# A gated recurrence and a cosine-gated layer on one core: order of sums, products and copies around the matmuls, and of the last group's tiles

## The chip, the core and the metric

The kernel runs on one NeuronCore of a Trainium2 chip. The engines work side by side, each through its own instructions in order, and wait for one another by semaphores: PE (TensorE, matmuls; its weight loads are shown apart as PEld), DVE (VectorE), ACT (ScalarE), POOL (GpSimd) and SP (SyncE, which here only issues DMAs). The metric is the device time of one execution in microseconds (us); lower is better. Three runs of the kernel before took 646.26, 646.23 and 644.99 us, the median is 646.23.

## The reference

```python
mag = np.sqrt(a_re * a_re + a_im * a_im)
scale = np.minimum(mag, 0.999) / (mag + 1e-06)
a_re_n, a_im_n = (a_re * scale, a_im * scale)
for t in range(S):                        # 768 steps, (batch 4, heads 8, 48 x 48 state)
    ar, ai = (a_re_n[:, :, t, :, None], a_im_n[:, :, t, :, None])
    new_re = ar * S_re - ai * S_im
    new_im = ar * S_im + ai * S_re
    kv = np.einsum('bhd,bhe->bhde', k[:, :, t], v[:, :, t])
    S_re, S_im = (new_re + kv, new_im)
    y[:, :, t] = np.einsum('bhd,bhde->bhe', q[:, :, t], S_re)
x = y.transpose(0, 2, 1, 3).reshape(3072, 384)
h = x @ w_in                              # 384 x 2048
g = h * np.cos(h)
out = g @ w_out                           # 2048 x 384
```

A recurrence with a complex decay per step and channel is followed by a layer with a cosine gate.

## The kernel before

The 3072 rows are cut into 24 chunks of 128 steps, two chunks to a group, so there are 12 groups g = 0 to 11; three groups make a batch, at whose start the recurrence begins anew (g = 0, 3, 6, 9). The first two groups and the weights' conversion are written out in order by hand; from group 2 on a loop over n runs, and only this loop and what follows it are touched here. One pass of it holds work of three groups at once:

- for group n + 1 the decays: `g_log`/`log_steps` (squares, logarithm, exponentials), `p_powers` (running sums of the logs on PE, `lgs`, then four exponentials on ACT into `lg` and `pair`, "the powers" below), `g_angle` (a table load and the arctangent on `tan`), `g_carry` (adds the angle of the chunk before, on DVE; not at a batch's start), `g_split` (`hi` on ACT, `lo` on DVE), `g_phase` (running sums of the angles on PE, `phs`), `g_trig`, `g_stack` (`ks`, `qs`), and `f_transpose` (`tr` on DVE, then through DRAM as `moved` into `kT` and `qT`). `p_end` halves the tile `end` and folds it into `least`, for a check at the program's end;
- for group n the scores `sc`, their masking into `atm` on DVE, the outputs `yp`, the state, and then the layer's first matmul in eight tiles of 256 columns of `w_in` (`first`, `mm1`);
- for group n - 1 the layer's second matmul, done as seven products of quarter matrices instead of eight (`seventh`, named a11, a12, s2, a22, s1, s3, s4 in this order on PE, 16 matmuls each). The mixes `s` and `gate<-gate` that they need are made on DVE. a11, s2, s1 and s4 add up in one PSUM tile, `sum`; after a11, s2, s1 (and s4, but in the last group) ACT copies its content out to `ot`, and the next of these products may write the tile only when that copy has read it. "The third sum's copy" is the one behind s2 (p == 3).

Five of the eight tiles (3 to 7) are computed as three products of rounded matrices, "three-product tiles": tiles 4 and 5 from group 3 on, 6 and 7 from group 4, 3 from group 5. They need `xT` cut into an upper part (`cut`, copied to `xh`), a lower part `xl` and a sum `xx` (`x_halves`: upper, lower, apart). For such a tile PE writes `hp` (xh times wh plus xl times wl) and `hb` (xx times wx); ACT copies `hb`, scaled, into `gate` (`cross_out`); DVE adds it onto `hp` (`whole_sum`, in the trace `hp<-hp,gate`); then come sine and square on ACT (`gate_sine`; `junk` is the square's output) and the product on DVE (`gate_product`, in the trace `gate<-hp,gate`). A plain tile has the sine, the square and the product alone. The gate part of a three-product tile is held back until the matmuls of the tile behind it are issued ("held").

What sets the order: `weave` sorts the steps of a pass by the place given to each between 0 and 1; a scheduler then orders each engine's instructions by that order and by readiness; `behind(a, b)` puts a behind b on their engine without a semaphore, and `chain` strings all instructions given to it on one engine, so the special functions on ACT stand in the order in which they are issued. PSUM tiles of `hp` rotate over three places, `hb`, `sc` and others over five.

Of the kernel before, what the change touches and what calls it, by code (L numbers as in the profile page):

```python
# [487 lines left out]
def fast_path(ctx, tc, q, k, v, a_re, a_im, moe_w_in, moe_w_out, out, least, odd, wide,  # L488
# [12 lines left out]
    G = 2  # L501
# [41 lines left out]
    def behind(ins, other):  # L543
        tc.add_manual_dep(ins.ins, other.ins.name, mybir.DependencyInfo(
            mybir.DependencyClass.NoSync, mybir.DependencyReason.DATA))
# [343 lines left out]

    def p_end(g, i, n):  # L890
        end = X[g]["end"][:, ds(i * H, n * H)]
        vector.tensor_scalar(out=end, in0=end, scalar1=-0.5, scalar2=None, op0=ALU.mult)
        low = least[:, ds(i * H, n * H)]
        vector.scalar_tensor_tensor(out=low, in0=end, scalar=LEAST, in1=low,
                                    op0=ALU.is_ge, op1=ALU.min)
# [265 lines left out]
    def x_halves(g):  # L1161

        x = X[g]

        def all_of():
            return x["xT"].rearrange("p c g t -> p (c g t)")

        def upper():
            whole = all_of()
            for name, tag in ("xx", "lg"), ("xl", "lo"), ("xh", "rs"):  # L1170
                x[name] = gt.tile([C, G * DM], F32R, tag=tag, name=name)
            x["cut"] = ft.tile([C, G * DM], F32, tag="yT", name="cut", bufs=1)
# [12 lines left out]
        def apart():  # L1185
            apart_ = vector.scalar_tensor_tensor(
                out=x["xx"], in0=x["xl"].bitcast(F32), scalar=-SHIFT,
                in1=x["cut"], op0=ALU.mult, op1=ALU.add)
            if g + 1 < NG:
                behind(apart_, x["product"])  # L1190

        return upper, lower, apart

    def three(g, jp):
        return g >= FROM.get(jp, NG)
# [67 lines left out]
    def mm1_gate(g, jp):  # L1263
        gate_sine(g, jp)
        gate_product(g, jp)

    def mm1(g, jp, last):

        mm1_sums(g, jp)
        if three(g, jp):  # L1270
            cross_out(g, jp)
        if "held" in X[g]:
            mm1_gate(g, X[g].pop("held"))
        if three(g, jp):
            X[g]["held"] = jp
            whole_sum(g, jp)
        else:
            mm1_gate(g, jp)
        if last:
            if g + 2 < NG:  # L1280
                X[g + 2]["steps"] = log_steps(g + 2, 0, G)
                next(X[g + 2]["steps"])
            if "held" in X[g]:
                mm1_gate(g, X[g].pop("held"))
# [68 lines left out]
    def seventh(g, p, part):  # L1353
# [19 lines left out]
        if g == NG - 1:  # L1373
            c12 = rest
        if p in (0, 3, 5) or p == 6 and not alone:
            late["scalar"] = scalar.mul(out={0: c11, 3: c21, 5: c22, 6: c12}[p], in_=ps, mul=scale)
        if g == NG - 1 and p == 5:
            scalar.mul(out=c12, in_=ps, mul=scale)
        for part_ in {1: [c11], 2: [c21], 4: [c21, c22], 6: [c12] * alone}.get(p, []):
# [44 lines left out]
    def keys(g):  # L1424

        if not 0 <= g < NG:
            return
        for i, n in spans(g):
            yield lambda i=i, n=n: g_trig(g, i, n)
            yield lambda i=i, n=n: (g_stack(g, i, n), p_end(g, i, n))  # L1430
            for name in "kT", "qT":
                if g >= PEG:
                    yield lambda i=i, n=n, name=name: f_transpose(g, i, n, name)
# [5 lines left out]
        return [lambda i=i: p_powers(g, i) for i in range(G)]  # L1439

    def prods(g):
        if not 0 <= g < NG:
            return
        if g not in (1, 2):
            yield from powers(g)
            yield lambda: g_angle(g, 0, G)
        if g <= PEG:
            yield lambda: (g_carry(g), g_split(g))
            yield lambda: (p_even(g, 0, G), p_apply(g, 0, G))
        else:  # L1450
            yield lambda: p_around(g)
# [36 lines left out]
    def first(g):  # L1488
        late_ = [jp for jp in THREE if FROM[jp] == g + 1]
        order = late_ + [jp for jp in range(NJ // 2) if jp not in late_]  # L1490
        if g == NG - 1:
            order = 0, 4, 1, 5, 2, 6, 7, 3
        return [lambda jp=jp: mm1(g, jp, jp == order[-1]) for jp in order]

    def second(g, i):
# [293 lines left out]
    for n in range(2, NG):  # L1789
        turned_keys, plain = list(keys(n + 1)), n == PLAIN  # L1790
        split = x_halves(n) if any(three(n, jp) for jp in THREE) else ()
        guard_ = list(guarded(n - 1, per)) if n > 2 else []
        convert = [lambda jp=jp: halves(jp) for jp in THREE if FROM[jp] == n + 1]
        if split and n < NG - 1:
            X[n + 1]["upper"] = split[0]
        weave((mixes(n - 1, 2, 4), 0.0, 0.08), (logs(n + 1), 0.0, 0.02), (chunks(n), 0.0, 0.36),
              (upper[2:] if plain else [], 0.0, 0.2), (products(n - 1, 0, 2 + (n < NG - 1)), 0.0, 0.365),
              (mixes_again(n - 1, "s3"), 0.06, 0.18), (mixes_again(n - 1, "s2"), 0.19, 0.27),
              (angles(n + 1), 0.2695, 0.2699), (prods(n + 1), 0.2701, 0.2735), (second(n - 1, 1), 0.36, 0.5),
              (mixes_again(n - 1, "s4"), 0.37, 0.48),  # L1800
              (products(n - 1, 2 + (n < NG - 1), 7), 0.4, 0.56),
              (convert[0:1], 0.82, 0.82), (convert[1:2], 0.93, 0.93),
              (phases(n + 1), *((0.472, 0.476) if plain else (0.476, 0.484))),
              (turned_keys[0:1], 0.5, 0.5), (split[0:1] if n == NG - 1 else [], 0.525, 0.525), (turned_keys[1:2], 0.53, 0.53),
              (turned_keys[2:3], 0.56, 0.56), (turned_keys[3:4], 0.6, 0.6), ([lambda: rest_of(n - 1)], 0.605, 0.605), (split[1:2], *[0.61 if n < NG - 1 else 0.53] * 2),
              (split[2:3], *[0.65 if n < NG - 1 else 0.54] * 2), (last_quarter() if plain else [], 0.9, 1.0), (first(n), 0.56, 1.0),
              (mixes(n, 0, 2 + (n == NG - 1)), 0.98 if convert else 0.92, 1.0 if n < NG - 1 else 0.97), (guard_[0:1], 0.1, 0.1),
              (guard_[1:2], 0.26, 0.26), (guard_[2:3], 0.47, 0.47))
    checked = verdict(late, temp)

    def judged():
        late["tensor"] = tail["tensor"]
        next(checked, None)

    weave(([judged], 0.0, 0.0), (mixes(NG - 1, 3, 4), 0.01, 0.1),
          (mixes_again(NG - 1, "s3"), 0.05, 0.15), (mixes_again(NG - 1, "s2"), 0.16, 0.26), (mixes_again(NG - 1, "s4"), 0.3, 0.4),
          (products(NG - 1, 0, 7), 0.0, 1.0), ([judged], 0.58, 0.6), ([judged], 0.76, 0.8))
    assert not guards
# [92 lines left out]
```

## Time and profile before

| | |
|---|---|
| median of three runs | 646.23 us |
| the profiled execution's own time | 647.06 us |
| its span, first to last instruction | 645.2 us |
| mean granted clock of PE | 0.997 |
| PE busy | 627.5 us, 97% |
| DVE busy | 529.7 us, 82% |
| ACT busy | 450.6 us, 70% |
| table load ahead of the arctangent, n = 7 and n = 8 | starts at 392.64 and 442.20 us |

All times of the trace are microseconds from the span's start. A row of the order of time gives start, duration, engine, line, operation, output <- inputs, shapes, how many instructions were merged, and in brackets how long the engine was idle before and what ended the wait. Many instructions share lines 681, 692 and 712, which are helpers that record every operation, so rows are told apart by their tiles. Two passes of the loop are 49.6 us apart by the table loads of the last row. A wait for several semaphores is put down to the one that came last by the profile.

### The profile page before, as it was taken

What the parts mean: (1) busy time and instruction counts of PE and PEld (TensorE: products, weight loads), DVE (VectorE), ACT (ScalarE), POOL (GpSimd) and SP (SyncE); (2) the same over time, 40 slices, a digit from 0 to 9 for tenths busy, and PEclk for the clock granted to TensorE, in tenths of its full rate; (3) what the DMA queues carried; (4) which work ended last, traced back from release to release, by engine and by line L of the source; (5) the groups of instructions that cost most, each with busy time, mean ns of one, the idle gap of its engine ahead of it and who ended that gap; (6) DMA issues with size and microseconds to landing.
All of it is one profiled execution on the core that took longest, in us unless ns stands there. A gap on an engine that the chain in (4) does not pass through costs nothing.

```text
span 645.2 us, 11446 instructions
## 1 busy us (share of the span) xinstructions
PE 627.5 (97%) x4321; PEld 573.0 (89%) x4321; DVE 529.7 (82%) x856; ACT 450.6 (70%) x812; POOL 30.3 (5%) x53
## 2 busy tenths in 40 slices
PE   8999999999999999999999999999999999999987
PEld 6788867777899999999999999999999899999987
DVE  6999989869798799898799799788889889973261
ACT  7888687285696696697598588588588589552430
POOL 4010200000010000000000000000000000000000
PEclk9999999999999999999999999999999999999989
DMA  9968655725926926946946945855865863641001
GB/s 229 247 190 217 195 172 117 179 49 135 208 65 158 245 74 157 224 112 148 236 108 148 221 124 148 199 145 140 187 165 130 190 162 109 150 97 50 25 2 31
DMA packets 232923, 94.94 MB, mean 147 GB/s; under 512 B 208701, under 2 KB 221246, under 8 KB 232858
## 3 DMA queue, kind: packets, MB, share of 16 engines
q1 hardware_dynamic: 225320, 68.51, 46.7%
q0 software_dynamic: 5824, 25.50, 12.0%
q8 instruction: 36, 0.59, 0.4%
q10 hardware_dynamic: 1714, 0.11, 0.2%
q14 instruction: 29, 0.24, 0.1%
HBM read 69.28 MB, written 24.81 MB: 146 GB/s over the span
## 4 chain that ended last, share of the span: by engine, by line
PE 46%; ACT 23%; DMA 12%; DVE 9%; issue 6%; SPq 2%; ACTq 0%; DVEq 0%
PE hp L692 16%; PE op L692 11%; PE sum L692 6%; PE sc L692 3%; PE hb L692 3%; DVE tr L681 2%; ACT rs L712 2%; ACT junk L681 2%; ACT tan L712 2%; PE yp L692 2%; DMA row<-lg 2%; ACT lg L712 2%; DMA k<-in_k_dram 2%; ACT raw L681 2%; ACT yT L681 2%
## 5 line engine op out<-in xcount | busy, mean ns | idle before, releaser
L692 PE MATMUL hp<-xT,w_in 128*128 128x256 f32 (+1 forms) x684 | 146.9, 372 | 0.7 <-DVE gate L681 0.7
L692 PEld LDWEIGHTS hp<-xT,w_in 128*128 128x128 f32 x684 | 125.9, 190 | 18.5 <-DVE gate L681 1.1
L712 ACT ACTIVATE gate<-hp,half_pi_b 128x512 f32<-128x512 f32 x96 | 65.9, 687 | 62.8 <-PE hp L692 40.8
L692 PE MATMUL op<-w_out,gate 128*128 128x192 f32 (+1 forms) x464 | 104.8, 377 | 0.0
L692 PEld LDWEIGHTS op<-w_out,gate 128*128 128x128 f32 x464 | 80.4, 193 | 16.7 <-issue 1.9
L692 PE MATMUL sum<-w_out,gate 128*128 128x192 f32 x304 | 54.9, 328 | 2.6 <-DVE gate L681 2.6
L681 ACT ACTIVATE junk<-hp 128x512 bf16<-128x512 f32 x96 | 56.7, 590 | 0.0
L681 DVE TENSOR_TENSOR gate<-hp,gate 128x512 f32<-128x512 f32 x55 | 37.6, 686 | 19.9 <-ACT junk L681 19.6
L692 PEld LDWEIGHTS sum<-w_out,gate 128*128 128x128 f32 x304 | 49.2, 190 | 2.9 <-DVE gate L681 2.9
L681 DVE SCALAR_TENSOR_TENSOR gate<-hp,gate 128x512 f32<-128x512 f32 x41 | 28.3, 691 | 27.3 <-ACT junk L681 27.2
L692 PE MATMUL sc<-qT,kT 96*128 96x128 f32 x384 | 48.9, 276 | 0.6 <-ACT gate L681 0.3
L692 PEld LDWEIGHTS sc<-qT,kT 96*128 96x128 f32 x384 | 46.8, 192 | 2.4 <-issue 0.6
L692 PE MATMUL hp<-xh,wh 128*128 128x256 f32 x246 | 44.2, 288 | 0.0
L692 PE MATMUL hp<-xl,wl 128*128 128x256 f32 x246 | 42.5, 281 | 0.0
L692 PE MATMUL hb<-xx,wx 128*128 128x256 f32 x246 | 35.7, 286 | 2.2 <-DVE xx L681 2.2
L681 DVE TENSOR_TENSOR gate<-gate 128x256 f32<-128x256 f32 x80 | 32.6, 418 | 5.4 <-PE op L692 4.8
L692 PEld LDWEIGHTS hp<-xh,wh 128*128 128x128 f32 x246 | 35.8, 189 | 0.5
L681 DVE TENSOR_TENSOR atm<-sc,causal 128x512 f32<-128x512 f32 x48 | 32.0, 683 | 4.8 <-PE sc L692 4.8
L681 ACT ACTIVATE ot<-sum 128x192 f32<-128x192 f32 x39 | 12.5, 320 | 32.5 <-PE sum L692 32.5
L692 PE MATMUL yp<-atm,v 128*48 128x128 f32 x352 | 34.0, 277 | 0.8 <-DVE atm L681 0.8
L692 PEld LDWEIGHTS hp<-xl,wl 128*128 128x128 f32 x246 | 34.8, 188 | 0.0
L681 DVE TENSOR_TENSOR hp<-hp,gate 128x512 f32<-128x512 f32 x41 | 28.4, 692 | 7.8 <-ACT gate L681 7.4
(163 smaller groups left out, 1262.3 us busy)
## 6 DMA issues: line engine op xcount, KB each, us to landing
moved<-tr SPq DMA_DIRECT2D x20, 768.0 KB
raw<-in_moe_w_in_dram POOLq DMA_DIRECT2D x16, 768.0 KB, 5.7
raw<-in_moe_w_out_dram POOLq DMA_DIRECT2D x16, 768.0 KB, 5.0
kT<-moved SPq DMA_DIRECT2D x40, 192.0 KB
qT<-moved SPq DMA_DIRECT2D x10, 768.0 KB
k<-in_k_dram SPq DMA_DIRECT2D x24, 192.0 KB
q<-in_q_dram SPq DMA_DIRECT2D x24, 192.0 KB
v<-in_v_dram SPq DMA_DIRECT2D x24, 192.0 KB
```

Of the source, the lines that this page charges most:

```text
L681: ins = getattr(self.engine, op)(**kw)
L692: chain(nc.tensor.matmul(out, **kw), "tensor")
L712: chain(nc.scalar.activation(func=func, **kw))
```

## The change

It has five parts.

- `mm1`: for a held three-product tile the sine and square are issued as before, but the next tile's sum (`whole_sum`) is issued ahead of the held tile's product, and the product is put behind that sum.
- `x_halves` and the loop: `apart` (xx) is no longer put behind the first product, and stands right behind `lower` (place 0.612 instead of 0.65). `p_end` moves from the stacking step to place 0.615, behind xx.
- `seventh`: the third sum's copy is chained on ACT in passes up to n = 10; to this end `prods` is split, and `carries` with the arctangent, the carry and the split is issued at 0.336 instead of 0.27.
- `first`: the last group's tiles run in the order 0 3 1 4 2 5 6 7 instead of 0 4 1 5 2 6 7 3.
- The mixes of the last group: two of the four are placed ahead of the loop's end instead of three.

```diff
     def p_end(g, i, n):
         end = X[g]["end"][:, ds(i * H, n * H)]
-        vector.tensor_scalar(out=end, in0=end, scalar1=-0.5, scalar2=None, op0=ALU.mult)
+        halved = vector.tensor_scalar(out=end, in0=end, scalar1=-0.5, scalar2=None, op0=ALU.mult)
+        if g > 0 and "apart" in X[g - 1]:
+            behind(halved, X[g - 1]["apart"])
...
-            if g + 1 < NG:
-                behind(apart_, x["product"])
+            x["apart"] = apart_
...
         if three(g, jp):
             cross_out(g, jp)
-        if "held" in X[g]:
-            mm1_gate(g, X[g].pop("held"))
+        held = X[g].pop("held", None)
+        if held is not None:
+            gate_sine(g, held)
         if three(g, jp):
             X[g]["held"] = jp
             whole_sum(g, jp)
-        else:
+        if held is not None:
+            gate_product(g, held)
+            if three(g, jp):
+                behind(X[g]["product"], X[g]["whole"])
+        if not three(g, jp):
             mm1_gate(g, jp)
...
-            late["scalar"] = scalar.mul(out={0: c11, 3: c21, 5: c22, 6: c12}[p], in_=ps, mul=scale)
+            late["scalar"] = copied = scalar.mul(out={0: c11, 3: c21, 5: c22, 6: c12}[p], in_=ps, mul=scale)
+            if p == 3 and g < NG - 2:
+                chain(copied)
...
-            yield lambda i=i, n=n: (g_stack(g, i, n), p_end(g, i, n))
+            yield lambda i=i, n=n: (g_stack(g, i, n), g > PEG or p_end(g, i, n))
...
     def prods(g):
+        return powers(g) if 0 <= g < NG else []
+
+    def carries(g):
         if not 0 <= g < NG:
             return
-        if g not in (1, 2):
-            yield from powers(g)
-            yield lambda: g_angle(g, 0, G)
+        yield lambda: g_angle(g, 0, G)
...
         if g == NG - 1:
-            order = 0, 4, 1, 5, 2, 6, 7, 3
+            order = 0, 3, 1, 4, 2, 5, 6, 7
...
-              (angles(n + 1), 0.2695, 0.2699), (prods(n + 1), 0.2701, 0.2735), (second(n - 1, 1), 0.36, 0.5),
+              (angles(n + 1), 0.2695, 0.2699), (prods(n + 1), 0.2701, 0.2735), (carries(n + 1), 0.336, 0.34), (second(n - 1, 1), 0.36, 0.5),
...
-              (split[2:3], *[0.65 if n < NG - 1 else 0.54] * 2), (last_quarter() if plain else [], 0.9, 1.0), (first(n), 0.56, 1.0),
-              (mixes(n, 0, 2 + (n == NG - 1)), 0.98 if convert else 0.92, 1.0 if n < NG - 1 else 0.97), (guard_[0:1], 0.1, 0.1),
+              (split[2:3], *[0.612 if n < NG - 1 else 0.54] * 2), ([lambda: p_end(n + 1, 0, G)] if n + 1 < NG else [], 0.615, 0.615), (last_quarter() if plain else [], 0.9, 1.0), (first(n), 0.56, 1.0),
+              (mixes(n, 0, 2), 0.98 if convert else 0.92, 1.0 if n < NG - 1 else 0.97), (guard_[0:1], 0.1, 0.1),
```

How the instructions stand on the engines follows from the scheduler as well. On DVE, in a pass of the loop from the cut of `xT` on (`gate<-hp,gate` with two operands is a plain tile's product or, as SCALAR_TENSOR_TENSOR, a three-product tile's; `hp<-hp,gate` is a sum), before:

```order
L681 TENSOR_SCALAR cut<-xT 128x768
L681 TENSOR_SCALAR end<-end 96x16
L681 SCALAR_TENSOR_TENSOR least<-end,least 96x16
L681 TENSOR_TENSOR gate<-hp,gate 128x512
L681 TENSOR_TENSOR xl<-xT,cut 128x768
L681 TENSOR_TENSOR gate<-hp,gate 128x512
L681 SCALAR_TENSOR_TENSOR xx<-xl,cut 128x768
L681 TENSOR_TENSOR gate<-hp,gate 128x512
L681 TENSOR_TENSOR hp<-hp,gate 128x512
L681 SCALAR_TENSOR_TENSOR gate<-hp,gate 128x512
L681 TENSOR_TENSOR hp<-hp,gate 128x512
```

and now, in the same place:

```order
L681 TENSOR_SCALAR cut<-xT 128x768
L681 TENSOR_TENSOR gate<-hp,gate 128x512
L681 TENSOR_TENSOR xl<-xT,cut 128x768
L681 SCALAR_TENSOR_TENSOR xx<-xl,cut 128x768
L681 TENSOR_SCALAR end<-end 96x16
L681 TENSOR_TENSOR gate<-hp,gate 128x512
L681 SCALAR_TENSOR_TENSOR least<-end,least 96x16
L681 TENSOR_TENSOR gate<-hp,gate 128x512
L681 TENSOR_TENSOR hp<-hp,gate 128x512 x2
L681 SCALAR_TENSOR_TENSOR gate<-hp,gate 128x512
```

xx has passed one product, the two instructions on `end` have left the way of xl, and the second sum has passed the first three-product tile's product.

On ACT, in a pass behind the powers, with the arctangent as `tan<-tan` and the third sum's copy as `ot<-sum` (a minus is before, a plus now):

```order
 L712 ACTIVATE lg<-lgs 128x384
 L712 ACTIVATE pair<-lgs 128x384
-L708 ACT_TABLE_LOAD
-L712 ACTIVATE tan<-tan 128x768
-L681 ACTIVATE ot<-sum 128x192
+L681 ACTIVATE ot<-sum 128x192
+L708 ACT_TABLE_LOAD
+L712 ACTIVATE tan<-tan 128x768
 L733 ACTIVATE hi<-tan 128x768
```

The copy has passed the table load and the arctangent; nothing else moved there.

On PE the rows are the same in kind all through. In the last group, behind the tiles, the first product (a11, into `sum`) and the second (a12, into `op`) read these gates, by number, where 5631 (before) and 5629 (now) is the gate of the tile that is computed last:

```order
 L692 MATMUL sum_5656<-w_out_125,gate_5470 128x192 x2
 L692 MATMUL sum_5656<-w_out_125,gate_5511 128x192 x2
 L692 MATMUL sum_5656<-w_out_125,gate_5550 128x192 x2
-L692 MATMUL sum_5656<-w_out_125,gate_5631 128x192 x2
-L692 MATMUL op_5675<-w_out_125,gate_5497 128x192 x2
+L692 MATMUL sum_5656<-w_out_125,gate_5497 128x192 x2
 L692 MATMUL op_5675<-w_out_125,gate_5536 128x192 x2
 L692 MATMUL op_5675<-w_out_125,gate_5575 128x192 x2
 L692 MATMUL op_5675<-w_out_125,gate_5598 128x192 x2
+L692 MATMUL op_5675<-w_out_125,gate_5629 128x192 x2
```

The last tile's gate has moved from the end of the first product to the end of the second.

More of the change, by code (lines that the diff above doesn't have):

```diff
@@ L1813, in judged @@
         next(checked, None)
-    weave(([judged], 0.0, 0.0), (mixes(NG - 1, 3, 4), 0.01, 0.1),
+    weave(([judged], 0.0, 0.0), (mixes(NG - 1, 2, 4), 0.0, 0.1),
           (mixes_again(NG - 1, "s3"), 0.05, 0.15), (mixes_again(NG - 1, "s2"), 0.16, 0.26), (mixes_again(NG - 1, "s4"), 0.3, 0.4),
```

## The prediction

> **What bounds the kernel now.** I read the page first, then who waits for whom on the weight-load track, then the order of time around each wait.
>
> ```profile
> span 645.2 us, 11446 instructions
> PE 627.5 (97%) x4321; PEld 573.0 (89%) x4321; DVE 529.7 (82%) x856; ACT 450.6 (70%) x812; POOL 30.3 (5%) x53
> ```
>
> PE is busy for 627.5 of 645.2 us, and the change leaves every matmul in place, so at most the 17.7 us of its idle time and time at a low clock can go. Which idle stretches there are, the weight loads (PEld, issued by the same sequencer) show best:
>
> ```profile
> PEld sum L692 <- ACT ot L681: 3.9, 5, 1.3
> PEld hb L692 <- DVE xx L681: 3.4, 6, 0.7
> PEld sum L692 <- DVE gate L681: 2.9, 1, 2.9
> PEld yp L692 <- DVE atm L681: 1.8, 4, 0.6
> PEld sc L692 <- ACT gate L681: 0.5, 1, 0.5
> ```
>
> The first three rows, 10.2 us, are the three places that the change edits: the third sum's copy `ot` (five waits), `xx` (six), and the last gate of the last group (one). Of the fourth row two of four waits, about 0.9 us, lie in the loops n = 6 and 9, which the change reaches; the fifth is the start of n = 11.
>
> **The tail (order 0 3 1 4 2 5 6 7).** In order of time, then the page's granted clock over the span and one stretch with it (the column behind POOL), then the page's groups for a sine, a square and a mix:
>
> ```profile
> 618.10 2.11 PE L692 MATMUL sum<-w_out,gate 128*128 128x192 f32 x12
> 620.00 0.69 DVE L681 TENSOR_TENSOR hp<-hp,gate 128x512 f32<-128x512 f32 x1
> 622.08 0.69 DVE L681 SCALAR_TENSOR_TENSOR gate<-hp,gate 128x512 f32<-128x512 f32 x1
> 622.83 0.92 PE L692 MATMUL sum<-w_out,gate 128*128 128x192 f32 x4 [2.62 <-DVE gate L681]
> 623.59 4.44 PE L692 MATMUL op<-w_out,gate 128*128 128x192 f32 x16
> 630.46 2.76 PE L692 MATMUL op<-t_a,gate 128*128 128x192 f32 x16
> PEclk9999999999999999999999999999999999999989
> 623.86:627.27 3.41, 3.41 (x13) 3.41 (x12) 1.25 (x3) 0.26 (x1) 0.00 (x0) 0.50 0.02 0
> L712 ACT ACTIVATE gate<-hp,half_pi_b 128x512 f32<-128x512 f32 x96 | 65.9, 687 | 62.8 <-PE hp L692 40.8
> L681 ACT ACTIVATE junk<-hp 128x512 bf16<-128x512 f32 x96 | 56.7, 590 | 0.0
> L681 DVE TENSOR_TENSOR gate<-gate 128x256 f32<-128x256 f32 x80 | 32.6, 418 | 5.4 <-PE op L692 4.8
> ```
>
> The first product takes 12 matmuls and then sits 2.62 us until tile 3's gate, the last of eight, is there at 622.77. One microsecond after PE resumes, the clock falls to 0.50 for 3.41 us, and a product of 16 matmuls lasts 4.44 instead of 2.76 us: 1.68 us more. In the new order the first product reads gates 0 to 3, all early, and runs through; the second reads gate 7 only in its last quarter. That quarter starts 16 + 12 matmuls behind 618.10; at 2.60 us for 16 (the n = 7 rows below, 32 in 5.20) this is 622.65. The last gate also comes earlier: its sum (0.69) no longer waits for the held product. The last tile's matmuls end about where the product starts, so its sum ends near 619.0, sine (0.69) and square (0.59) take until 620.3, and the product until about 621.4 with two mixes in its queue. That is 1.2 us of room. Behind it stand the mixes for the third product (0.42 each, some seven of them, to about 624.4), whose last quarter is read at 618.10 + 44/16 × 2.60 = 625.25. So the gap goes and nothing replaces it: **2.62 + 1.68 = 4.3 us**. The end stays PE's, since the rest of the tail is products back to back. Bounds: 2.6 if the clock falls all the same, 4.5 with the 0.1 to 0.2 us that a restart costs.
>
> [...]
>
> **The third sum's copy.** In loop n = 8, PE's and ACT's rows and DVE's part in it:
>
> ```profile
> 438.26 2.76 PE L692 MATMUL sum<-t_s,gate 128*128 128x192 f32 x16
> 442.20 1.28 ACT L708 ACT_TABLE_LOAD   x1
> 443.50 0.84 ACT L712 ACTIVATE tan<-tan 128x768 f32<-128x768 f32 x1
> 444.25 0.31 ACT L681 ACTIVATE ot<-sum 128x192 f32<-128x192 f32 x1
> 444.61 2.87 PE L692 MATMUL sum<-t_s,s 128*128 128x192 f32 x16 [0.99 <-ACT ot L681]
> 445.32 0.96 DVE L681 SCALAR_TENSOR_TENSOR lo<-tan,hi 128x768 fp32r<-128x768 f32 x1 [0.37 <-ACT hi L733]
> 447.49 0.34 PE L692 MATMUL phs<-lo,exact 128*128 128x384 f32 x1
> ```
>
> The s2 product ends at 441.02, its copy starts only behind table load and arctangent, and the s1 product, which adds into the same PSUM tile, waits 0.99 us. Moved ahead of the table load the copy ends near 442.5 at the latest, before the a22 product is through at 443.6: the wait goes, 1.1 us with the restart. The price is 0.31 us on the arctangent's chain (arctangent, carry, hi, lo, then `phs` on PE). Here lo is finished at 446.28, and PE, earlier by 1.1, asks for it at 446.4: just in time. That holds in n = 5 and 8. Where a batch goes on, PE is later and the picture is another (n = 7):
>
> ```profile
> 390.02 2.76 PE L692 MATMUL sum<-t_s,gate 128*128 128x192 f32 x16
> 392.64 1.28 ACT L708 ACT_TABLE_LOAD   x1
> 394.81 0.62 DVE L681 SCALAR_TENSOR_TENSOR tan<-tan,carry 32x384 f32<-32x384 f32 x1 [0.53 <-ACT tan L712]
> 395.22 2.76 PE L692 MATMUL sum<-t_s,s 128*128 128x192 f32 x16
> ```
>
> There PE didn't wait. The product ends at 392.78, so the copy, chained, can't start before 392.84; the table load moves from 392.64 to 393.17, and with it arctangent and carry, for which DVE already waits 0.53 us: **0.53 us later** on that chain in n = 4, 7 and 10, with nothing gained. In n = 3, 6 and 9 the wait was small (row one's other three), and lo takes most of it back.
>
> **xx behind xl, and the sum ahead of the product.**
>
> ```profile
> 460.39 0.94 DVE L681 TENSOR_TENSOR xl<-xT,cut 128x768 fp32r<-128x768 f32 x1
> 461.70 0.69 DVE L681 TENSOR_TENSOR gate<-hp,gate 128x512 f32<-128x512 f32 x1 [0.37 <-ACT junk L681]
> 462.31 0.95 DVE L681 SCALAR_TENSOR_TENSOR xx<-xl,cut 128x768 fp32r<-128x768 f32 x1
> 463.31 1.69 PE L692 MATMUL hb<-xx,wx 128*128 128x256 f32 x12 [0.40 <-DVE xx L681]
> ```
>
> xx now starts with xl's end, 461.33 instead of 462.31, and the two small instructions on `end` ahead of xl (0.3 us) move behind it: 1.2 us earlier against a wait of 0.2 to 0.7. The product in between becomes about 0.7 us later; PE needs its PSUM tile only for the second three-product tile, over 1.7 us behind `hb`'s start, so this hides.
>
> ```profile
> 472.34 0.51 PE L692 MATMUL hp<-xl,wl 128*128 128x256 f32 x3
> 475.66 0.69 DVE L681 TENSOR_TENSOR hp<-hp,gate 128x512 f32<-128x512 f32 x1
> 477.75 1.28 ACT L708 ACT_TABLE_LOAD   x1
> ```
>
> Tile 7's matmuls end at 472.85 and its sum runs at 475.66, 2.8 us later, because each sum stands behind the held tile's product, which stands behind a sine and a square that need the sum before. With the sum first, each step of that chain loses a product. I get the last sum right behind the matmuls and the first table load about 1.6 us earlier. ACT and DVE so start their long stretch (logs to transposes) earlier, which covers the late `atm` (0.9 us) and the arctangent's 0.31 us. What is queued behind a sum is the held product alone; it is needed two tiles of 2.1 us later.
>
> **What is late next** is the transfer of the transposed queries. For n = 10:
>
> ```profile
> 557.08 2.23 DVE L681 STREAM_TRANSPOSE tr<-qs 128x1536 f32<-128x1536 f32 x1
> 571.00:572.00 1.00, 0.89 (x8) 0.69 (x6) 0.59 (x1) 0.87 (x3) 0.00 (x0) 1.00 0.67 242
> 572.00:573.00 1.00, 0.80 (x7) 0.83 (x8) 1.00 (x3) 0.20 (x1) 0.00 (x0) 1.00 0.05 18
> 572.16 0.52 PEld L692 LDWEIGHTS sc<-qT,kT 96*128 96x128 f32 x4 [0.47 <-ACT gate L681]
> ```
>
> The DMA share (last but one column) falls to 0.05 just where the next scores `sc` start after waiting: the transfer of 13 us behind the transposes has no room there, and the ACT instruction named had ended at 571.87. A loop's gain counts only as far as the transposes come earlier too. No view shows the room in the other loops, so it is bounded from nothing to the whole wait. My reading: n = 5 and 8, where phs and everything behind it come about a microsecond earlier, keep 3.1 us together (1.1 and 0.5 each); n = 6 and 9 2.0; n = 4, 7 and 10, with their later arctangent, 0.5; n = 3 nothing. **5.6 us**, with bounds of 0 and 8.7 (rows one, two and five, and half of row four: 3.9 + 3.4 + 0.5 + 0.9). Loop 2 and all before it are untouched.
>
> **Sum.** 4.3 + 5.6 = 9.9 us. The profiled execution took 647.06 us, its span of 645.2 and 1.86 around it, and would take 637.2; the median shown, 646.23, is 0.83 below it, so **636.3 us**.
>
> **Rivals.**
> 1. All waits go, the transfer isn't in the way: 8.7 + 4.3 = 13.0, time 633.2. For it: xx and the long stretch both come over a microsecond earlier. Against: the rows of n = 10. 0.18.
> 2. The loops give nothing, since the later arctangent and the transfer eat it, and only the tail remains: 641.9. For it: n = 7's rows. Against: n = 5 and 8, whose products are done early. 0.13.
> 3. The half-speed stretch doesn't come from the gap, and stays though the gap goes: 1.7 more, 638.0. For it: the gap is shorter than the stretch. Against: it begins 1.03 us behind the gap, and no earlier slice of the profile's row shows one. 0.08. [...]
> 4. Slower: the copy is now a barrier between PE and ACT. If the s2 product, whose mixes DVE does later in the new order, ends 0.54 us or more behind the powers in all eight loops, arctangent, transposes and transfer are 0.85 us later in each, and where the transfer bounds the loop: 8 × 0.85 − 4.3 = 2.5 longer, 648.7. The point from which it decides is 4.3 / 8 = 0.54 us a loop. In n = 8 the product ends 1.2 us ahead of the table load behind the powers, in n = 7 0.14 after its start. 0.04.
> 5. The edits don't act where the waits are, or one undoes another: within 0.2% of before (1.3 us, about what a measurement of this kernel can tell from no change). The instruction order shows that they act. 0.03.
>
> My forecast has 0.54. The range of 633.2 to 641.0 takes in rival 3, the near part of 1 and the upper half of the loops' bounds; it leaves out rivals 4 and 5, most of 2 and the far part of 1, under 0.2 in all. Faster is 0.54 + 0.18 + 0.13 + 0.08 = 0.93, the same 0.03, slower 0.04.
>
> **What would show it.** The tail is right if the first product runs 16 matmuls without a wait and the clock stays at 1.00 to the end. The copy is right if `sum <- ACT ot` is gone and the arctangent in n = 7 starts about 0.5 us later behind its product. The sum is right if the first table load of a loop comes 1.5 us sooner after the last tile; xx, if `hb <- DVE xx` is gone. The reservation is right if new waits stand at `sc` with no engine late, and at `phs` for lo. A longer wait for a PSUM tile at `hp` would prove the whole wrong.

## The result, and the profile after

The changed kernel takes **635.96 us** (median of four runs, 635.52 to 637.05) against 645.61 (four runs, 644.63 to 646.26) of the kernel before: a ratio of 0.9854, 95% interval 0.9834 to 0.9875. The forecast was 636.3 us, with a range of 633.2 to 641.0. In a later set it took 636.05 us against 646.64.

The profiled execution took 635.72 us. From its page, the span, the busy times and the granted clock over the span:

```profile
span 633.8 us, 11436 instructions
...
PE 623.4 (98%) x4321; PEld 571.4 (90%) x4321; DVE 530.4 (84%) x856; ACT 450.2 (71%) x812; POOL 30.2 (5%) x53
...
PEclk9999999999999999999999999999999999999999
```

The span is 11.3 us shorter, and PE's idle share is down from 17.7 to 10.4 us. The dip of the clock at the end is gone, and PE is 4.1 us less busy with the same 4321 matmuls. Of the rows on which the change was worked out, and what has come, this is what its weight loads wait for now (waited for, us in total, times, longest):

```profile
PEld phs L692 <- DVE lo L681: 2.2, 7, 0.6
...
PEld yp L692 <- DVE atm L681: 0.6, 1, 0.6
```

The three rows that the change was put at (`sum <- ot` 3.9, `hb <- xx` 3.4, `sum <- gate` 2.9) are gone, and `yp <- atm` fell from four waits to one, which lies ahead of n = 3. One row has grown, from 0.2 us: `phs` waits for `lo`, 0.56 us in n = 3 and 0.28 or 0.29 in each of n = 4, 6, 7, 9 and 10.

Where the 11.3 us lie, from the starts of the first scores `sc` of each pass (175.24 and 572.20 for n = 3 and n = 11 before, 175.06 and 564.74 now), the last matmul's end (641.03, now 628.94) and the span: 0.2 ahead of n = 3, **7.3 in the loops**, **4.6 in the tail** (from n = 11 to the last matmul, 68.83 to 64.20), and **0.75 lost** behind the last matmul (4.15 to 4.90). One pass, in us:

| n | 3 | 4 | 5 | 6 | 7 | 8 | 9 | 10 |
|---|---|---|---|---|---|---|---|---|
| before | 49.93 | 49.65 | 49.26 | 49.56 | 49.56 | 49.49 | 49.58 | 49.93 |
| changed | 49.87 | 49.81 | 47.68 | 48.24 | 49.14 | 47.57 | 48.24 | 49.14 |

The tail, in order of time (start, duration, engine, line, operation): PE's two first products, and DVE's last sum and last gate product.

```profile
610.58 2.76 PE L692 MATMUL sum<-w_out,gate 128*128 128x192 f32 x16
610.90 0.69 DVE L681 TENSOR_TENSOR hp<-hp,gate 128x512 f32<-128x512 f32 x1
613.11 0.68 DVE L681 SCALAR_TENSOR_TENSOR gate<-hp,gate 128x512 f32<-128x512 f32 x1
613.17 2.76 PE L692 MATMUL op<-w_out,gate 128*128 128x192 f32 x16
```

The first product runs its 16 matmuls in one piece, and the last gate ends at 613.79, 1.3 us ahead of the matmul that reads it (16 + 12 matmuls behind 610.58).

The start of a pass, n = 9, which stands against the forecast's rows of tile 7:

```profile
467.01 0.51 PE L692 MATMUL hp<-xl,wl 128*128 128x256 f32 x3
...
467.63 0.70 DVE L681 TENSOR_TENSOR hp<-hp,gate 128x512 f32<-128x512 f32 x1
...
470.58 1.28 ACT L708 ACT_TABLE_LOAD   x1
```

The last sum follows the matmuls in 0.1 us instead of 2.8, and the first table load starts 3.22 us behind the first scores instead of 5.06.

### The profile page after: what moved, and what is told of

It reads as the page before. It is cut to its first block, busy times and chain, and to the rows that moved or that the text cites. A ratio compares the mean times of both kernels' runs of the same rounds, so it can differ in the third digit from the quotient of the medians.

```text
span 633.8 us, 11436 instructions
## 1 busy us (share of the span) xinstructions
PE 623.4 (98%) x4321; PEld 571.4 (90%) x4321; DVE 530.4 (84%) x856; ACT 450.2 (71%) x812; POOL 30.2 (5%) x53
## 4 chain that ended last, share of the span: by engine, by line
PE 92%; ACT 3%; DVE 3%; issue 1%; DMA 1%; SPq 0%; DVEq 0%
PE hp L692 30%; PE op L692 19%; PE sum L692 16%; PE sc L692 7%; PE yp L692 6%; PE hb L692 5%; PE sp L692 4%; PE phs L692 2%; PE lgs L692 2%; PE yr L692 1%; PE tp L1006 1%; DMA im<-in_a_im_dram 1%; ACT tan L712 1%; DVE tan L681 0%; ACT lg L712 0%
## 5 line engine op out<-in xcount | busy, mean ns | idle before, releaser
L692 PE MATMUL op<-w_out,gate 128*128 128x192 f32 (+1 forms) x464 | 103.2, 372 | 0.0
L692 PEld LDWEIGHTS op<-w_out,gate 128*128 128x128 f32 x464 | 78.7, 190 | 16.7 <-issue 1.9
L681 DVE TENSOR_TENSOR gate<-hp,gate 128x512 f32<-128x512 f32 x55 | 37.6, 685 | 18.4 <-ACT junk L681 17.7
L681 ACT COPY yT<-yp 48x512 f32<-48x512 f32 x44 | 25.4, 577 | 16.5 <-PE yp L692 16.0
L681 ACT ACTIVATE gate<-hb 128x512 f32<-128x512 f32 x41 | 24.5, 599 | 14.7 <-PE hb L692 14.0
```

The source lines that it names most:

```text
L681: ins = getattr(self.engine, op)(**kw)
L692: chain(nc.tensor.matmul(out, **kw), "tensor")
```

## The experiments

Eleven runs were made beside the two kernels. The profiles and times of all, with what the rows below rest on: the first scores of n = 11, the weight loads' waits in total, the time from there to the last matmul's end (tail), and behind that end: how long before it the flag was there, how long ACT took to issue the last store, and the time to the span's end. All us.

| kernel | median | span | sc, n = 11 | sum<-ot | hb<-xx | phs<-lo | tail | flag ahead | store issue | end |
|---|---|---|---|---|---|---|---|---|---|---|
| before | 645.61 | 645.2 | 572.20 | 3.9 | 3.4 | 0.2 | 68.83 | 6.9 | 0.39 | 4.15 |
| changed | 635.96 | 633.8 | 564.74 | 0 | 0 | 2.2 | 64.20 | 3.6 | 1.66 | 4.90 |
| e1 order alone | 643.76 | 642.4 | 571.49 | 4.1 | 3.1 | 0.4 | 64.51 | 3.3 | 2.93 | 6.39 |
| e2 without order | 636.52 | 634.4 | 564.62 | 0 | 0 | 2.2 | 65.70 | 6.1 | 0.39 | 4.13 |
| e3 without sum | 639.37 | 636.7 | 567.20 | 0 | 0 | 3.3 | 64.51 | 3.1 | 1.73 | 4.95 |
| e4 without copy | 635.07 | 632.8 | 563.98 | 0.6 | 0 | 0.2 | 64.20 | 4.7 | 1.13 | 4.67 |
| e5 without xx | 640.01 | 637.7 | 568.41 | 0 | 3.5 | 2.2 | 64.26 | 4.2 | 1.32 | 4.99 |
| e6 flag early | 635.73 | 634.2 | 565.18 | 0 | 0 | 2.2 | 64.27 | 6.9 | 0.39 | 4.76 |
| e7 sum alone | 637.68 | 635.6 | 565.86 | 0.6 | 2.0 | 0.2 | 65.62 | 6.1 | 0.40 | 4.14 |
| e8 copy alone | 646.50 | 643.2 | 572.02 | 0 | 3.6 | 3.3 | 67.08 | 5.8 | 0.39 | 4.13 |
| e9 copy in n = 3, flag early | 634.35 | 632.5 | 564.12 | 0 | 0 | 0.9 | 64.19 | 6.9 | 0.39 | 4.16 |
| e10 changed again | 636.05 | 634.2 | 565.15 | 0 | 0 | 2.2 | 64.27 | 3.9 | 1.25 | 4.78 |
| e11 without copy again | 635.60 | 633.2 | 563.93 | 0.6 | 0 | 0.4 | 64.20 | 4.4 | 1.43 | 5.12 |

Beside them the kernel before took 646.57 us (e1 to e4), 645.95 (e5 to e8) and 646.64 (e9 to e11). Two profiles of the changed kernel differ by 0.4 us in the fourth column, those without the copy by 0.05, and e1, which edits nothing in the loops, stands 0.7 from before; loop differences smaller than that are not read.

### The tail: the order alone, and everything but the order

e1 is the kernel before with the order of the last group's tiles (and the placement of its mixes); e2 is the changed kernel with both undone.

```diff
-            order = 0, 4, 1, 5, 2, 6, 7, 3
+            order = 0, 3, 1, 4, 2, 5, 6, 7
...
-              (mixes(n, 0, 2 + (n == NG - 1)), 0.98 if convert else 0.92, 1.0 if n < NG - 1 else 0.97), (guard_[0:1], 0.1, 0.1),
+              (mixes(n, 0, 2), 0.98 if convert else 0.92, 1.0 if n < NG - 1 else 0.97), (guard_[0:1], 0.1, 0.1),
...
```

> The kernel before with one part of the change alone: the last group's tiles in the order 0 3 1 4 2 5 6 7, and two of its mixes ahead of the loop's end instead of three. My theory: the gap of 2.62 us goes (at most 0.3 us of it comes back at the second product's last quarter, since the last gate is as late as before), and with it the half-speed stretch; the span falls by 4.0 to 4.3 us, to about 641. Rival (the clock falls for another reason than the gap): the half-speed stretch stays, the span falls by 2.6 us at most, to 642.6.

> The changed kernel with the old order 0 4 1 5 2 6 7 3 and the old places of the mixes. My theory: the loops run as in the changed kernel; in the tail the sum ahead of the product brings the last gate 1.2 to 1.6 us sooner, so a gap of 1.0 to 1.4 us is left in the first product. If the clock falls behind any gap of about a microsecond there, the half-speed stretch comes back and the span is about 636.6; if it takes a longer one, the clock stays at 1.00 and the span is about 635.0. Rival (the loops' gain hangs on the tail's order): the span goes back to 640 or more.

e1: ratio 0.9973 (0.9943 to 1.0003; one of its ten runs took 652.38 us, which widens the interval). The tail is 4.3 us shorter as forecast, without gap and without a stretch at half speed, but 2.2 of it are given back behind the last matmul, where the last store takes 2.93 us to issue (below). So the edit that is worth 4.3 us on PE is worth 2.8 in the time by itself, by the medians (646.57 to 643.76).

e2: ratio 0.9855 (0.9834 to 0.9875), as much as the whole change. Its first products in order of time, and a window behind the gap (length, busy times of PE, PEld, DVE, ACT, POOL, granted clock, DMA share, GB/s):

```profile
610.53 2.11 PE L692 MATMUL sum<-w_out,gate 128*128 128x192 f32 x12
613.80 0.92 PE L692 MATMUL sum<-w_out,gate 128*128 128x192 f32 x4 [1.15 <-DVE gate L681]
...
614.00:617.50 3.50, 3.50 (x23) 3.50 (x23) 3.22 (x12) 0.33 (x1) 0.00 (x0) 1.00 0.02 0
```

The sum ahead of the product alone brings the last gate 1.5 us closer, and behind this gap of 1.15 us the clock stays at 1.00. Of the tail's gain 3.1 us come with the sum too (68.83 to 65.70), and the new order adds 1.5 to that. In the time it adds 0.6 (636.52 to 635.96, not told apart by the intervals), since the end is 0.77 longer.

### The sum: all but it, and it alone

```diff
-        held = X[g].pop("held", None)
-        if held is not None:
-            gate_sine(g, held)
+        if "held" in X[g]:
+            mm1_gate(g, X[g].pop("held"))
         if three(g, jp):
             X[g]["held"] = jp
             whole_sum(g, jp)
-        if held is not None:
-            gate_product(g, held)
-            if three(g, jp):
-                behind(X[g]["product"], X[g]["whole"])
-        if not three(g, jp):
+        else:
             mm1_gate(g, jp)
```

This is e3's edit of the changed kernel; e7 is the same edit turned round, made to the kernel before.

> The changed kernel with the next tile's sum behind the held tile's product again. My theory: the sum ahead of the product is what brings ACT and DVE their lead; without it the first table load of a loop goes back from 3.2 to 5.1 us behind the first scores, the arctangent comes 0.3 us later than in the kernel before, waits of phs for lo grow, and about 3 us of the loops' gain is lost: span about 637. Rival (ACT and DVE were not in the way, the copy and xx alone took the waits away): span within 0.5 us of the changed kernel's 633.8.

> The kernel before with one part of the change alone: the next three-product tile's sum ahead of the held one's product. xx, the copy and the last group's order as before. Theory (this part does most of the work, and the copy's wait goes with it because table load and arctangent come 1.8 us earlier): first table load of a loop at sc + 3.2 instead of 5.06 from n = 6 on, sum <- ot gone in n = 5 and 8 without the copy's part, hb <- xx waits stay (0.2 to 0.7 each), the tail's gap 1.15 us with the clock at 1.00, span 634.5 to 636.5. Rival (the parts need one another, as the forecast had it: the copy gives n = 5 and 8 their microsecond): sum <- ot stays near 1 us in n = 5 and 8, span above 638.

e3: 0.9899 (0.9878 to 0.9919); the loops lose 2.5 us against the changed kernel, and the first table load is back at 5.06 us behind the scores. e7: 0.9883 (0.9854 to 0.9912); alone the part takes 6.3 us out of the loops and 3.2 out of the tail. Its wait for the copy is down to one of 0.6, in n = 3, though the copy still stands behind the arctangent. The wait's row, and then pass n = 8, in order of time:

```profile
PEld sum L692 <- ACT ot L681: 0.6, 1, 0.6
...
437.74 1.28 ACT L708 ACT_TABLE_LOAD   x1
...
439.03 0.84 ACT L712 ACTIVATE tan<-tan 128x768 f32<-128x768 f32 x1
...
439.79 0.31 ACT L681 ACTIVATE ot<-sum 128x192 f32<-128x192 f32 x1
...
440.76 2.44 PE L692 MATMUL sum<-t_s,s 128*128 128x192 f32 x14
```

The copy ends at 440.10, 0.66 us ahead of the product that needs the tile. The theory holds: **this part carries most of the change**, and the forecast's reason for n = 5 and 8 (that the copy must be moved) does not.

### The copy: all but it, and it alone

e4 undoes the copy's part of the changed kernel; e8 makes it in the kernel before.

```diff
-            late["scalar"] = copied = scalar.mul(out={0: c11, 3: c21, 5: c22, 6: c12}[p], in_=ps, mul=scale)
-            if p == 3 and g < NG - 2:
-                chain(copied)
+            late["scalar"] = scalar.mul(out={0: c11, 3: c21, 5: c22, 6: c12}[p], in_=ps, mul=scale)
...
-        yield lambda: g_angle(g, 0, G)
+        if g not in (1, 2):
+            yield from powers(g)
+            yield lambda: g_angle(g, 0, G)
...
```

> The changed kernel without the chained copy: the third sum's copy stands behind the arctangent again, and the arctangent, carry and split are issued at 0.27 as before. The prediction held the copy to be worth 1.1 us in each of n = 5 and 8: then the waits of s1 for the copy come back and the span is about 636. The trace of the changed kernel makes me doubt that: with the lead of the sum the arctangent would be over before s1 asks for the copy, and the copy now holds the arctangent back by 0.4 to 1.0 us in every loop (phs waits for lo 2.2 us in seven loops). By this theory the span is 1 to 2 us shorter than the changed kernel's 633.8.

> The kernel before with one part of the change alone: the third sum's copy ahead of table load and arctangent. Theory (the forecast's): the wait sum <- ot of 0.99 us goes in n = 5 and 8 and those loops keep about 1.1 us each, n = 4, 7 and 10 have their arctangent 0.53 us later and lose at most 0.2 each, n = 6 and 9 keep 0.2 to 0.4; the tail as before, with gap and half speed; span 643.0 to 644.0 against 645.2. Rival (the wait only moves from the copy to lo, which is just in time): waits phs <- lo of up to 0.5 us in all loops, span 645.0 or more.

e8: ratio 1.0028 (0.9995 to 1.0061), and with 0.2 us out of the loops no change there that can be told: the copy's waits are gone (3.9 to 0), `phs <- lo` has come in their place (0.2 to 3.3), and a transfer of `xT` is now waited for in n = 5 and 8 (1.1 together). The rival holds in the loops; the span is shorter by 2.0 us for another reason, the clock (last section). e4: 0.9832 (0.9812 to 0.9852), 1.0 us less span than the changed kernel. Pass n = 7, the changed kernel first, then e4:

```profile
387.04 2.76 PE L692 MATMUL sum<-t_s,gate 128*128 128x192 f32 x16
...
389.83 0.33 ACT L681 ACTIVATE ot<-sum 128x192 f32<-128x192 f32 x1 [0.64 <-PE sum L692]
...
390.18 1.28 ACT L708 ACT_TABLE_LOAD   x1
...
394.15 0.95 DVE L681 SCALAR_TENSOR_TENSOR lo<-tan,hi 128x768 fp32r<-128x768 f32 x1
...
395.15 0.44 PE L692 MATMUL phs<-lo,exact 128*128 128x384 f32 x1
```

```profile
389.20 1.28 ACT L708 ACT_TABLE_LOAD   x1
...
391.24 0.31 ACT L681 ACTIVATE ot<-sum 128x192 f32<-128x192 f32 x1
...
392.23 2.76 PE L692 MATMUL sum<-t_s,s 128*128 128x192 f32 x16
...
393.16 0.95 DVE L681 SCALAR_TENSOR_TENSOR lo<-tan,hi 128x768 fp32r<-128x768 f32 x1
...
395.00 0.34 PE L692 MATMUL phs<-lo,exact 128*128 128x384 f32 x1
```

The bracket in the first fence is the price: ACT sits idle 0.64 us for PE's product, because the chained copy may not be passed, and the table load starts 0.98 us later than in e4, lo 0.99, `phs <- lo` 0.15 (0.09 of each was there at the pass's first scores). In e4 the copy ends at 391.55, 0.7 us ahead of the product that needs the tile. With the sum first, the old place is early enough in every pass but n = 3 (a gap of 0.33 us on PE there).

### xx: all but it

```diff
-            x["apart"] = apart_
+            if g + 1 < NG:
+                behind(apart_, x["product"])
...
-            yield lambda i=i, n=n: (g_stack(g, i, n), g > PEG or p_end(g, i, n))
+            yield lambda i=i, n=n: (g_stack(g, i, n), p_end(g, i, n))
...
-              (split[2:3], *[0.612 if n < NG - 1 else 0.54] * 2), ([lambda: p_end(n + 1, 0, G)] if n + 1 < NG else [], 0.615, 0.615), (last_quarter() if plain else [], 0.9, 1.0), (first(n), 0.56, 1.0),
+              (split[2:3], *[0.65 if n < NG - 1 else 0.54] * 2), (last_quarter() if plain else [], 0.9, 1.0), (first(n), 0.56, 1.0),
```

> The changed kernel with its xx part undone: xx is again behind the first product on DVE and the two small instructions on `end` stand ahead of xl again. Theory (xx alone sets hb): in the changed kernel xx ends 0.91 us ahead of hb in n = 5 and 8 (sc + 37.38 against 38.29 in n = 8) and 0.4 to 0.6 us ahead in n = 6, 7, 9 and 10; 1.2 us later, the waits hb <- xx come back with 0.3 us (n = 5, 8) and 0.6 to 0.8 us (n = 6, 7, 9, 10), 3.4 us in all, and the span grows from 633.8 to about 637.2. Rival (the waits come back, but the long stretch of ACT and DVE behind takes them up, since the table load depends on the last tile's sum and not on hb): waits of the same size, the span 635 at most.

Ratio 0.9913 (0.9886 to 0.9941). The waits come back with 3.5 us, where 3.4 were expected, and the loops lose 3.7 (3.3 against the second profile of the changed kernel), so nothing behind them takes them up: the theory holds. e5 in n = 6, in order of time:

```profile
359.31 0.94 DVE L681 TENSOR_TENSOR xl<-xT,cut 128x768 fp32r<-128x768 f32 x1
360.63 0.69 DVE L681 TENSOR_TENSOR gate<-hp,gate 128x512 f32<-128x512 f32 x1 [0.38 <-ACT junk L681]
361.24 0.95 DVE L681 SCALAR_TENSOR_TENSOR xx<-xl,cut 128x768 fp32r<-128x768 f32 x1
...
362.24 0.97 PE L692 MATMUL hb<-xx,wx 128*128 128x256 f32 x6 [0.60 <-DVE xx L681]
```

In the changed kernel the same rows are

```profile
359.02 0.94 DVE L681 TENSOR_TENSOR xl<-xT,cut 128x768 fp32r<-128x768 f32 x1
359.99 0.96 DVE L681 SCALAR_TENSOR_TENSOR xx<-xl,cut 128x768 fp32r<-128x768 f32 x1
...
361.38 0.88 PE L692 MATMUL hb<-xx,wx 128*128 128x256 f32 x6
```

xx starts 1.25 us earlier and has 0.4 us of room. e5 against e7, neither of which has the xx part (they differ beside the copy only in the tail's order), shows what the copy's part costs where there is no such room: the loops of e5, with it, are 2.5 us longer than those of e7, where `hb <- xx` is 2.0 instead of 3.5. The late arctangent delays the transposes on DVE, and with them cut, xl and xx: in n = 6, behind the first scores, the arctangent starts at 19.92 us against 19.01, the first transpose at 31.25 against 30.58, xx at 38.81 against 38.14 and `hb` at 39.82 against 39.14. So the 3.7 us hold part of the copy's price. Without the copy's part xx is worth less: e4, which has xx, stands 1.9 us ahead of e7, which hasn't, at the first scores of n = 11 (563.98, 565.86), and neither has the copy's part.

### The end of the program, and a version that beats both

e6 is the changed kernel with two small transfers of the final check sent straight to the line that is reduced, without a row in DRAM between.

```diff
-        line_d = scratch.tile([D2 + C], F32, name="line_d")
-        behind(nc.sync.dma_start(out=line_d[0:D2], in_=low.rearrange("p o -> (p o)")),
-               late["x"])
-        nc.sync.dma_start(out=line_d[D2:D2 + C], in_=even.rearrange("p o -> (p o)"))
         line = temp("lg")[0:1, 0:D2 + C]
-        late["line"] = nc.sync.dma_start(out=line, in_=line_d.unsqueeze(0))
+        behind(nc.sync.dma_start(out=line[:, 0:D2], in_=low.rearrange("p o -> (p o)")),
+               late["x"])
+        late["line"] = nc.sync.dma_start(out=line[:, D2:D2 + C], in_=even.rearrange("p o -> (p o)"))
```

> The changed kernel with one edit at the program's end: the two small tiles of the check (`low` and `even`) go straight into the line that is reduced, in one transfer each, instead of through a row in DRAM and back. Nothing of the loop or the products is touched. The flag is then there about 4 us earlier, near 621.2 instead of 625.18, 7.7 us ahead of the last matmul's end instead of 3.8. Theory (the later the flag against the last matmul, the longer the end, because the engines then read flag and branch at the same time as the last store is issued): the time from the last matmul's end to the span's end falls from 4.90 to about 4.15 us, as before the change, the issue of the last store on ACT from 1.66 to 0.39 us, and the span to 633.1. Rival (the long store issue has nothing to do with the flag): 4.9 us again, span 633.8.

Half of it came: the flag is there 6.9 us ahead of the last matmul's end and the store is issued in 0.39 us, but the end is 4.76 us, and the time (0.9842, 0.9815 to 0.9870) is not told apart from the changed kernel's. e9 joins this edit with the copy's part kept in n = 3 alone (PLAIN is 2); e10 and e11 are the changed kernel and e4 again, beside it on the same chip.

```diff
-            if p == 3 and g < NG - 2:
+            if p == 3 and g == PLAIN:
...
+        yield from powers(g)
+        if g != PLAIN + 2:
+            yield lambda: g_angle(g, 0, G)
...
-        yield lambda: g_angle(g, 0, G)
+        if g == PLAIN + 2:
+            yield lambda: g_angle(g, 0, G)
...
```

> The changed kernel without the copy's part in all passes but n = 3 (where its absence brought a wait of 0.33 us), and with the flag's two small tiles sent straight into the line that is reduced. Theory (the copy costs time wherever the sum goes first, and the late flag lengthens the issue of the last store): the loops as in the kernel without the copy but n = 3 some 0.2 us shorter, the first scores of n = 11 at 563.8, the last store issued in 0.39 us, span 632.0 to 632.6, median about 634.3. Rival (only the profile that was looked at differed, and copy and flag are worth nothing): the same median as the changed kernel within 0.3 us.

> The changed kernel as it is, on the same chip as the two others, for a comparison of their times. Theory (the copy's part costs time here): 1.0 us longer than the kernel without the copy, 1.6 us longer than the one that has the flag early as well. Rival: all three within 0.3 us.

> The changed kernel with the copy's part undone everywhere, on the same chip. Theory: 0.9 us under the changed kernel, 0.5 us above the one with the copy in n = 3 alone and the flag early. Rival: all three within 0.3 us.

e9 took **634.35 us** (633.57 to 634.57; ratio 0.9817, 0.9794 to 0.9840), e11 635.60 (635.12 to 635.94), the changed kernel 636.05 (635.20 to 638.04). No run of e9 is as long as the shortest of the other two, so it beats both by 1.3 to 1.7 us. The copy's part by itself costs 0.45 us by these medians, where 0.9 was expected; the runs overlap, and why it is less is open (the two profiled executions, 636.08 and 635.12, lie 0.96 apart). In the loops it costs 1.2 (565.15 against 563.93), and 0.8 between the changed kernel and e4. Kept in n = 3 alone it buys nothing there: a wait of 0.62 us for the copy (e4) has become one of 0.56 for lo, and the first scores of n = 11 are no earlier (564.12). So in the profiles the lead of e9 over e11 is the end's, 4.16 us against 5.12. The last rows of e9, the flag on DVE and the store on ACT, and then those of the changed kernel:

```profile
621.28 0.14 DVE L1875 TENSOR_SCALAR flag<-bad 1x1 int32<-1x1 f32 x1
...
628.81 0.39 ACTq L1403 DMA_DIRECT2D out_dram<-rest  x1
```

```profile
625.18 0.14 DVE L1872 TENSOR_SCALAR flag<-bad 1x1 int32<-1x1 f32 x1
...
629.43 1.66 ACTq L1403 DMA_DIRECT2D out_dram<-rest  x1
```

## Why the prediction was right, and where it was not

- **The tail, 4.3 forecast, 4.6 measured.** Right step by step: no gap, no half-speed stretch, the last gate 1.3 us early where 1.2 were worked out, and 0.27 for the restart (12 and 4 matmuls took 2.11 + 0.92 us, 16 in one piece take 2.76), so a little over the bound of 4.5. e1 shows it alone. The 1.68 us of the clock are there only in executions of the kernel before in which the clock falls, 23 of 37 (last section).
- **The loops, 5.6 forecast, 7.3 measured.** A term too small in size in each group: n = 5 and 8 gave 3.5 (3.1), n = 6 and 9 2.7 (2.0), n = 4, 7 and 10 together 1.05 (0.5), n = 3 0.1 (0). The step that was too careful is the reservation: what was held back was held for the transfer of the transposed queries, and it took back tenths only. The weight loads' named waits in these passes (those over 0.3 us a row) came to 9.3 us before (0.5, 0.23 and 0.5 of `atm` in n = 6, 8 and 9 among them) and are 2.0 now, all `phs <- lo`. In the changed kernel, n = 10, the second transpose, and two stretches ahead of the first scores at 564.74 (DMA share in the last column but one):

```profile
550.25 2.24 DVE L681 STREAM_TRANSPOSE tr<-qs 128x1536 f32<-128x1536 f32 x1
...
563.00:564.00 1.00, 1.00 (x10) 1.00 (x10) 1.00 (x2) 0.56 (x3) 0.00 (x0) 1.00 0.99 347
564.00:565.00 1.00, 1.00 (x11) 1.00 (x10) 0.93 (x3) 1.00 (x3) 0.00 (x0) 1.00 0.10 32
```

The transpose starts 6.8 us earlier than before and the scores 7.5, and the transfer is still through by 564, 0.7 us ahead. The transfer moves with the transposes and took no longer (from the second transpose's start, 557.08, to between 571 and 572 before, from 550.25 to 564 now). It has little room, though. In the second profile of this kernel (e10) the weight loads of the scores wait 0.25 us at the start of n = 8 and 0.29 at that of n = 11 (565.12), and the DMA share falls from 1.01 to 0.36 in the half microsecond before the latter. e9 waits 0.49 us, from 274.41, at the first scores of n = 5 with no engine late; that this is the transfer is not shown.
- **The copy, right in what it does, wrong in what it is worth.** `sum <- ot` went, the arctangent in n = 7 starts 0.52 us later behind the scores than before (0.53 forecast), and `phs` waits for lo, as said. That was the price against the kernel before; with the sum first ACT could start the table load earlier, and against e4 the copy holds it back by 0.9 to 1.0 us in each of n = 6 to 10. But the microsecond in n = 5 and 8 was put down to it, and e7 gets it without: the sum brings the first table load 1.84 us earlier (1.6 forecast), and table load and arctangent are through before the product wants the tile. Two parts were each counted as the cure of one wait. With the first in place the second costs 0.8 to 1.2 us in the loops, and alone (e8) it moves the wait to lo.
- **xx, right**: `hb <- xx` is gone, worth 3.7 us beside the other parts (e5), the copy's price included. That the product in between hides was right too: no wait for a PSUM tile at `hp` has come.
- **The end, missing from the sum.** The forecast ended at the last matmul. The shorter tail leaves the check less cover, and 0.75 us go there, 2.2 in e1.
- **The sum of it all.** The spans differ by 11.3 us where 9.9 were forecast: 1.7 more in the loops, 0.3 in the tail, 0.2 ahead of n = 3, less 0.75 at the end. That the median came within 0.4 us of 636.3 is in part luck: the loops gave 1.7 us more than forecast, the end took 0.75 of it back, and the medians lie 9.7 apart in that set and 10.6 in the last.

Of the rivals, the first (all waits gone, 633.2) is the nearest: e9, with its copy and flag mended, is at 634.35. The second (only the tail) fell with the loops' 7.3 us, the third (the clock falls all the same) with the row of the clock, the fifth with everything. The fourth, the copy as a barrier between PE and ACT, names a mechanism that is there (the idle 0.64 us of ACT). Its delay of the arctangent came, 0.9 to 1.0 us against e4 where the rival had 0.85, but it costs at most 0.25 us a pass in the changed kernel against e4, and 0.5 in e10 against e11. Where xx has no room it comes near the rival's price: n = 6, 7, 9 and 10 are 0.6 to 0.75 us longer in e5 than in e7.

Not tried: xx in the kernel before without sum and copy.

## What to carry to other kernels

When two edits are aimed at one wait, work out each with the other in place: the one that moves a whole chain earlier can make the other a cost. An instruction that is chained ahead of a table load or another long step makes that step wait for its own input; look at when that input comes, in every pass and not only where the wait is. And a tail that gets shorter uncovers what ran beside it: follow the last small transfers and flags to the program's end as well. Where a gap on PE costs the clock in some executions only (here one of 2.62 us, in 23 of 37 by the mean clocks), one profile shows one of two prices; look at the clock of several.

## What was not expected of the hardware

**The clock does not always fall.** The same gap as before stands in e8, in order of time, with a window that holds the stretch behind it:

```profile
617.85 2.11 PE L692 MATMUL sum<-w_out,gate 128*128 128x192 f32 x12
622.58 0.92 PE L692 MATMUL sum<-w_out,gate 128*128 128x192 f32 x4 [2.62 <-DVE gate L681]
623.34 2.76 PE L692 MATMUL op<-w_out,gate 128*128 128x192 f32 x16
...
623.60:627.00 3.40, 3.40 (x23) 3.40 (x22) 2.37 (x6) 0.27 (x1) 0.00 (x0) 1.00 0.08 5
```

The gap is 2.62 us as in the kernel before, the clock stays at 1.00, and the product behind it takes 2.76 us and not 4.44. Of 37 executions of the kernel before that ran beside the experiments, 23 have a mean granted clock of 0.997 or less and a median span of 645.1 us, 14 one of 0.998 or more and 642.75. So behind one and the same gap the clock falls in some executions and not in others, going by these mean clocks, about 1.7 us apart by the profile's rows and 2.35 by the medians. Behind 1.15 or 1.16 us (e2, e7) the profiles show no fall.

Why the clock falls behind one of these gaps and not behind the other is not shown. In the kernel before it falls to 0.50 at 623.86, for 3.41 us. The gap, the stretch from its end to the fall, and the one behind the half speed (second number: PE busy; third from the end: the clock):

```profile
620.21:622.83 2.62, 0.00 (x1) 0.00 (x1) 2.56 (x7) 1.26 (x3) 0.00 (x0) 1.00 0.00 0
622.83:623.86 1.03, 1.03 (x6) 1.03 (x7) 1.00 (x6) 0.07 (x1) 0.00 (x0) 1.00 0.00 0
...
627.27:630.30 3.03, 3.03 (x20) 3.03 (x19) 1.11 (x3) 0.00 (x0) 0.00 (x0) 1.00 0.05 5
```

In the changed kernel, without the gap, the clock falls only behind the last matmul's end at 628.94:

```profile
629.00:631.60 2.60, 0.00 (x0) 0.00 (x0) 0.36 (x1) 0.00 (x0) 0.00 (x0) 1.00 0.07 21
631.60:633.84 2.24, 0.00 (x0) 0.00 (x0) 0.00 (x0) 0.00 (x0) 0.00 (x0) 0.51 0.16 48
```

**The last store's issue takes 0.39 us or several times that.** In the table, where the flag is there 5.8 us or more ahead of the last matmul's end, ACT issues it in 0.39 or 0.40 us (six profiles); where it is 4.7 us or less, in 1.13 to 2.93 (seven). All but e6 of the first kind end 4.13 to 4.16 us behind the last matmul, the second kind 4.67 to 6.39. e6 changed nothing but the two small transfers ahead of the flag, and the issue followed (0.39 us against 1.66 and 1.25), so the flag's time decides it as far as one profile can show. What lies between is in the traces: ACT reads the flag and branches (at 636.40 in the kernel before, at 625.88 in the changed one), and its next instruction comes 2.4 to 3.1 us behind the branch (638.96 and 628.92). In the six profiles with the short issue the store is issued 2.49 us or more behind that instruction (2.56 in the kernel before), in the seven with a long one 1.88 us or less (0.51 in the changed kernel, 0.14 in e1). Why the issue took longer there is not shown. Nor is why e6 still ended 4.76 us behind the last matmul: its span goes on for 3.88 us behind the store's issue, where the five others have 3.24 to 3.27.
